# The first batch of an attention and mixture-of-experts kernel, taken by head groups

## The chip, the cores and the metric

The kernel runs on one core of a Trainium2 chip. The metric is the device time of one execution in microseconds (us). PE is TensorE, DVE is VectorE, ACT is ScalarE, POOL is GpSimd, and SP is the sync engine, which issues nearly all loads here.

## The reference

Three stages follow each other on 4 batches of 576 tokens with 8 heads of 64:

```
# 1. attention over 32 memory slots, per batch and head
a   = softmax over the 576 tokens of phi            # (576, 32)
k_m = a^T k ;  v_m = a^T v                          # (32, 64) each
att = softmax over the 32 slots of (q k_m^T / 8)    # (576, 32)
x   = att v_m                                       # heads side by side: 2304 x 512
# 2. dense MLP: h = x w_in ; x = (h * sigmoid(h)) w_out        (512 -> 2048 -> 512)
# 3. mixture of 8 experts, two per token: relu(x w1[e]) w2[e], weighted and summed
```

## The kernel before

The whole program is one stream of instructions per engine. The Python code names the steps; a scheduling layer sets each engine's order once, when the program is built, and `tc.issue_after` keeps a step from standing ahead of a named one. At run time every engine takes its own stream in order, and each instruction waits there for what it needs.

**Head groups.** Heads are taken in pairs `r` = 0 to 3. The index `g` splits the 8 heads in two groups of four, `g` = 0 and 1 (pairs 0, 1 and pairs 2, 3; the change's title calls them even and odd). Work on the 32 slots of four heads fills 128 partitions, so each step of attention comes as one piece per group.

**Batch 0 is the prologue.** For each group `phi_top` takes a maximum over token chunks (DVE, tile `mx`), `phi_max` finishes it through PE transposes (`mt`), subtracts it (DVE) and takes the exponential (ACT). `memory` multiplies it with keys and values (tile `kv`, and `kx` for the last, half chunk; 20 PE matmuls a group), sums the weights into `rs` and writes the scaled result to `src`. `memory_t` transposes `src` of both groups on PE into `kvt`. `scores` multiplies `kvt` with the queries `q`, two PSUM buffers (tag `aux`, of which there are two in all) for two groups; DVE transposes them into `sct`. `softmax_a` and `softmax_b` do the softmax (`smx`, `ssm`), `turn` transposes back (`att`), `halves` splits the result into a rounded part and a rest (both named `ah`). Tokens come in two ranges: 256 columns and 320 columns (`T0`, `TW`).

**The weights.** They arrive as 64-bit floats and are turned into 32-bit ones by ACT (`lw` and `wi` or `wo`) and two DVE steps, `join` (L217) and `sign` (L221); the raw pieces sit in four buffers `st`. `project` multiplies v_m into a slice of `w_in` (PE, `wph`, `wpl`), which saves the product with v_m later. `mlp_h` and `mlp_x` (L288, L313) are the dense MLP, in 32 steps a batch; the pieces of `w_in` and `w_out`, and the attention of the next batch, are hung on these steps by number.

**SP's queue.** Loads are issued in the order phi (both groups), kv and kx (pairs 0 to 3), the first 256 columns of q, two pieces of `w_in`, the rest of q, then further weights. A load also waits for the one eight places ahead of it and for its buffer.

Of the kernel before, what the change touches and what calls it, by code (L numbers as in the profile page):

```python
# [44 lines left out]
def body(ctx, tc, a):  # L45
# [36 lines left out]
    src = const.tile([128, 2, 2, 64], F32, name="src")  # L82

    def load_phi(b):
        PH[b] = ap_.tile([SC, NCH, 256], F32, name="phi", tag="big", bufs=1)
        if b:
            sp.dma_start(PH[b], a["phi"][b])
        else:
            load_phi_part(b, 0)
# [25 lines left out]
    def phi_max(b, g):
        r = slice(g * 128, (g + 1) * 128)
        pt = psum("aux", 2)
        pe.transpose(pt[:, :SC], MX.pop((b, g)), ident)
# [8 lines left out]
        return last

    def memory(b, g):
        pk = psum("aux", 2)  # L130
# [8 lines left out]
        dve.reciprocal(rs, rs)
        v, w = src[:, :, g, :], pk[:, :128].rearrange("p (t d) -> p t d", t=2)  # L140
        if b == 0:
            act.activation(v, w, AF.Copy, scale=rs)
        else:
            dve.tensor_scalar(v, w, rs, None, op0=OP.mult)

    def memory_t(b):
# [12 lines left out]
    def scores(b, i):  # L159
        t0, w = T0[i], TW[i]  # L160
        p = [psum("aux", 2)[:, :w] for g in range(2)]
        heads(p, b, 0, lambda h: QT[b, h][:, t0:t0 + w])
        if i == 0:
            AT[b] = ap_.tile([128, 2, S // M, M], F32, name="sct", tag="big", bufs=1)
        for g in range(2):
            dve.transpose(AT[b][:, g].rearrange("p a m -> p (a m)")[:, t0:t0 + w], p[g])

    def softmax_a(b, t0, w):
        n = w // M
        t = AT[b][:, :, t0 // M:t0 // M + n, :]  # L170
        mx = ap_.tile([128, 2, S // M], F32, name="smx")[:, :, :n]
# [5 lines left out]
    def softmax_b(b, t0, w):
        n = w // M
        t = AT[b][:, :, t0 // M:t0 // M + n, :]
        sm = ap_.tile([128, 2, S // M], F32, name="ssm")[:, :, :n]  # L180
# [844 lines left out]
def layout(inputs, np):  # L1025
# [45 lines left out]
```

## Time and profile before

| | |
|---|---|
| median of 3 runs | 845.61 us (845.02 to 845.68) |
| the profiled execution's own time | 845.91 us |
| its span, first to last instruction | 844.1 us |
| PE busy | 807.1 us, 96% of the span |
| DVE busy | 496.8 us, 59% |
| ACT busy | 360.8 us, 43% |
| POOL busy | 209.9 us, 25% |
| mean granted TensorE clock | 0.983 |
| DMA | 137.84 MB, 163 GB/s over the span |

The span divided in 40 slices of 21 us shows where PE is not full: in the first two slices its digits are 4 and 5, later 8 and 9. The granted clock (PEclk) reads 5 and 9 in the first two slices, then 9, the highest digit, throughout.

### The profile page before, as it was taken

The numbers are of one execution on the slowest core, as the hardware profiler recorded it, in microseconds if no ns is written. First come the engines' busy times: TensorE is split into PE (matmuls) and PEld (weight loads), VectorE is DVE, ScalarE is ACT, GpSimd is POOL, SyncE is SP. The second block draws the span as 40 slices with busy tenths as digits, with TensorE's granted clock in tenths as the row PEclk, the third lists the DMA queues.
The fourth block names the chain that finished last, engine by engine and source line by source line (L and its number), as shares of the span: only waits on it lengthen the run. The fifth ranks groups of instructions, "written<-read, shape, count | busy, mean of one in ns | idle before, by whom it ended". The sixth has DMA issues, their size and how long they took to land.

```text
span 844.1 us, 14185 instructions
## 1 busy us (share of the span) xinstructions
PE 807.1 (96%) x5260; PEld 691.4 (82%) x5260; DVE 496.8 (59%) x1178; ACT 360.8 (43%) x856; POOL 209.9 (25%) x237
## 2 busy tenths in 40 slices
PE   4589999999999999999999999999999999999996
PEld 2267678878887888887988989989989899898995
DVE  4898996884268747655724555354553654546521
ACT  3689975444333454553414433324332333233410
POOL 1254530021000400400541504215133142241301
PEclk9599999999999999999999999999999999999999
DMA  9889852543074215232456893765748647586201
GB/s 304 291 295 325 283 217 71 159 131 94 7 229 153 51 51 151 57 82 50 113 138 187 257 257 124 185 237 171 188 169 221 241 139 160 198 220 196 74 4 53
DMA packets 85935, 137.84 MB, mean 163 GB/s; under 512 B 14045, under 2 KB 48349, under 8 KB 85856
## 3 DMA queue, kind: packets, MB, share of 16 engines
q1 hardware_dynamic: 74656, 104.41, 40.9%
q0 software_dynamic: 11200, 32.43, 12.7%
q8 instruction: 43, 0.70, 0.4%
q14 instruction: 36, 0.29, 0.1%
HBM read 106.13 MB, written 31.26 MB: 163 GB/s over the span
## 4 chain that ended last, share of the span: by engine, by line
PE 81%; DVE 9%; ACT 4%; DMA 3%; issue 2%; POOL 1%; SPq 0%; POOLq 0%; ACTq 0%; DVEq 0%
PE x L706 25%; PE x L313 18%; PE x L682 13%; PE h L682 12%; PE h L288 9%; PE aux L157 2%; DMA st<-moe_w_out 1%; DVE th L293 1%; DVE gl L298 1%; DMA kx<-kx 1%; ACT lw L211 1%; POOL wo L232 1%; DMA st<-moe_w_in 1%; DVE mx L113 1%; DVE wo L217 1%
## 5 line engine op out<-in xcount | busy, mean ns | idle before, releaser
L706 PE MATMUL x<-w,gh 128*128 128x512 f32 (+1 forms) x608 | 188.1, 390 | 0.0
L706 PEld LDWEIGHTS x<-w,gh 128*128 128x128 f32 (+1 forms) x608 | 112.4, 186 | 24.3
L682 PE MATMUL h<-xh,w 128*128 128x304 f32 (+4 forms) x512 | 118.7, 304 | 0.0
L706 PE MATMUL x<-w,gl 128*128 128x512 f32 (+1 forms) x304 | 118.5, 390 | 0.0
L682 PE MATMUL x<-xh,w 128*128 128x304 f32 (+4 forms) x512 | 118.1, 302 | 0.0
L288 PE MATMUL h<-ah,wph 128*128 128x320 f32 (+1 forms) x512 | 109.3, 302 | 3.8 <-DVE th L293 1.7
L313 PE MATMUL x<-gh,woh 128*128 128x512 f32 x256 | 105.5, 412 | 0.0
L288 PEld LDWEIGHTS h<-ah,wph 128*128 128x128 f32 x512 | 90.0, 192 | 18.2 <-ACT ah L195 3.6
L721 POOL DMA_INDIRECT out<-y,tab x40 | 41.9, 1049 | 243.1 <-DVE y L716 187.3
L313 PE MATMUL x<-gl,woh 128*128 128x512 f32 x256 | 100.7, 393 | 0.7 <-DVE gl L298 0.7
L313 PE MATMUL x<-gh,wol 128*128 128x512 f32 x256 | 101.2, 395 | 0.0
L293 DVE SCALAR_TENSOR_TENSOR th<-th,h 128x256 f32<-128x256 f32 (+1 forms) x128 | 57.6, 450 | 53.0 <-ACT th L291 52.5
L497 POOL DMA_INDIRECT tab_d<-rows,slot x36 | 40.6, 1128 | 191.3 <-DVE slot L494 177.9
L682 PEld LDWEIGHTS h<-xh,w 128*128 128x128 f32 x512 | 87.3, 188 | 0.6
L682 PEld LDWEIGHTS x<-xh,w 128*128 128x128 f32 x512 | 87.4, 188 | 0.0
L291 ACT ACTIVATE th<-h 128x256 f32<-128x256 f32 (+1 forms) x128 | 52.3, 408 | 73.4 <-PE h L288 71.3
L288 PE MATMUL h<-ah,wpl 128*128 128x256 f32 (+1 forms) x256 | 76.6, 300 | 2.3 <-DVE wpl L264 2.3
L682 PE MATMUL x<-xl,w 128*128 128x304 f32 (+4 forms) x256 | 78.0, 305 | 0.0
L682 PE MATMUL h<-xl,w 128*128 128x304 f32 (+4 forms) x256 | 77.7, 303 | 0.0
L297 ACT ACTIVATE gh<-th 128x256 fp32r<-128x256 f32 x128 | 53.3, 416 | 55.7 <-DVE th L293 55.3
L298 DVE TENSOR_TENSOR gl<-th,gh 128x256 fp32r<-128x256 f32 x120 | 55.1, 459 | 32.0 <-ACT gh L297 28.1
L716 DVE SCALAR_TENSOR_TENSOR y<-x,tab,ex 128x512 f32<-128x512 f32 (+2 forms) x35 | 26.2, 749 | 71.4 <-PE x L706 71.4
(189 smaller groups left out, 1342.0 us busy)
## 6 DMA issues: line engine op xcount, KB each, us to landing
w2s<-moe_w SPq DMA_DIRECT2D x32, 512.0 KB, 8.5
wi<-win_d SPq DMA_DIRECT2D x24, 512.0 KB, 5.1
w1s<-moe_w SPq DMA_DIRECT2D x24, 512.0 KB, 6.2
kv<-kv SPq DMA_DIRECT2D x16, 520.0 KB, 7.3
st<-moe_w_in SPq DMA_DIRECT2D x16, 512.0 KB, 5.2
st<-moe_w_out SPq DMA_DIRECT2D x16, 512.0 KB, 5.9
xs_d<-ex SPq DMA_DIRECT2D x25, 256.0 KB, 3.6
x_d<-xs SPq DMA_DIRECT2D x36, 128.0 KB, 2.4
```

Of the source, the lines that this page charges most:

```text
L157: pe.matmul(p[g][h * M:(h + 1) * M], KVT[b][r, t, h * M:(h + 1) * M], moving(h)[r], start=True, stop=True)
L288: pe.matmul(p[:, :w], wt[:, g, c:c + 128], AH[b, g][at][:, t0:t0 + w], start=(n == 0), stop=(n == 5))
L291: act.activation(th[:, :w], p[:, :w], AF.Tanh, scale=0.5)
L293: dve.scalar_tensor_tensor(u[:, :w], th[:, :w], 1.0, p[:, :w], op0=OP.add, op1=OP.mult)
L297: act.activation(gh, u[:, :256], AF.Copy)
L298: last = (pool if b == 0 and (2 * f + i) % 4 == 0 else dve).tensor_sub(gl, u[:, :256], gh.bitcast(F32))
L313: pe.matmul(X2[key], held, moved, start=(f == 0 and n == 0), stop=(f == NF - 1 and n == 2))
L497: st = pool.indirect_dma_start(out=tab_d, out_offset=bass.IndirectOffsetOnAxis(ap=slot[:, j, k:k + 1], axis=0), in_=rows.bitcast(I32)[:, j ...
L682: pe.matmul(p[:, :w], wt[:, d, c], x[:, d, r], start=(n == 0), stop=(n == 11))
L706: mm = pe.matmul(p, g, w[:, f, :], start=(n == 0), stop=(n == (15 if both else 23)))
L716: done = dve.scalar_tensor_tensor(y, p[:P], w, EX[k, j], op0=OP.mult, op1=OP.add)
L721: st = pool.indirect_dma_start(out=a["out"], out_offset=bass.IndirectOffsetOnAxis(ap=TAB[k][:P, j, 0:1], axis=0), in_=y, in_offset=None, b ...
```

## The change

Batch 0 is taken group by group. SP's order becomes phi of group 0, kv and kx of pairs 0 and 1, phi of group 1, the first columns of q, kv and kx of pairs 2 and 3; the rest follows as before. phi lies group by group in memory, so that a half is one run of 2560 bytes per partition (before: five of 512). `memory_t`, `scores`, `softmax_a` and `softmax_b` take a list of groups; for the first 256 tokens they are called once per group, and group 0's softmax, `turn` and `halves` stand ahead of group 1's `memory`. The conversion of the first piece of `w_in` (`shrink`, `join`, `sign`) now stands behind group 1's `memory_t`. The scores of batch 0 use phi's buffer. Later batches load phi in two DMAs instead of one.

```diff
     load_phi(0)
+    for r in range(2):
+        load_kv(0, r)
     load_phi_part(0, 1)
     for r in range(4):
+        load_q(0, r, 0, T0[1])
+    for r in range(2, 4):
         load_kv(0, r)
-    for r in range(4):
-        load_q(0, r, 0, T0[1])
     fetch_win(0)
...
-    for g in range(2):
-        phi_top(0, g)
-        phi_max(0, g)
+    phi_top(0, 0)
+    phi_max(0, 0)
+    with tc.issue_after(MX["sub"].ins):
+        phi_top(0, 1)
     memory(0, 0)
-    memory(0, 1)
+    phi_max(0, 1)
+    memory_t(0, (0,))
+    scores(0, 0, (0,))
+    softmax_a(0, T0[0], TW[0], (0,))
+    softmax_b(0, T0[0], TW[0], (0,))
+    turned = turn(0, 0, T0[0], TW[0])
+    with tc.issue_after(turned.ins):
+        ready = memory(0, 1)
+    with tc.issue_after(ready.ins):
+        ready = halves(0, 0, T0[0], TW[0])
     first = ST.pop(("i", 0))
     WI[0] = m1.tile([128, 4, PW], F32, name="wi", tag="wi", bufs=2)
     parts = [WI[0][:, 2 * g:2 * g + 2, :].rearrange("p r f -> p (r f)") for g in range(2)]
-    narrow(first[0], parts[0], True)
-    memory_t(0)
-    scores(0, 0)
-    low = shrink(first[1], parts[1])
-    with tc.issue_after(softmax_a(0, T0[0], TW[0]).ins):
+    with tc.issue_after(ready.ins):
+        ready = memory_t(0, (1,))
+    turned = ready
+    with tc.issue_after(turned.ins):
+        low = shrink(first[0], parts[0])
+    scores(0, 0, (1,))
+    topped = softmax_a(0, T0[0], TW[0], (1,))
+    with tc.issue_after(topped.ins):
+        join(parts[0], low)
+    sign(first[0], parts[0])
+    with tc.issue_after(turned.ins):
+        low = shrink(first[1], parts[1])
+    with tc.issue_after(topped.ins):
         joined = join(parts[1], low)
     sign(first[1], parts[1])
     pool.dma_start(win_d[0], WI[0].rearrange("p r f -> p (r f)"))
     with tc.issue_after(joined.ins):
-        softmax_b(0, T0[0], TW[0])
-    turn(0, 0, T0[0], TW[0])
+        softmax_b(0, T0[0], TW[0], (1,))
     turned = turn(0, 1, T0[0], TW[0])
     project(0, 1)
-    halves(0, 0, T0[0], TW[0])
     ready = halves(0, 1, T0[0], TW[0])
```

The order of three engines shows it. On DVE, before, from the phi maxima to the first scores; `mx` is the maximum over chunks, `mt` the finished one, `rs` the sums of `memory`:

```order
L113 TENSOR_REDUCE mx<-phi 128x128 x2
L120 TENSOR_REDUCE mt<-aux 128x1
L125 TENSOR_TENSOR phi<-phi,aux 128x2x128
L125 TENSOR_TENSOR phi<-phi,aux 128x3x128
L120 TENSOR_REDUCE mt<-aux 128x1
L125 TENSOR_TENSOR phi<-phi,aux 128x2x128
L125 TENSOR_TENSOR phi<-phi,aux 128x3x128
L138 TENSOR_SCALAR rs<-aux 128x1
L139 RECIPROCAL rs<-rs 128x1
L138 TENSOR_SCALAR rs<-aux 128x1
L139 RECIPROCAL rs<-rs 128x1
```

The same place on DVE now (line numbers shift by a few; the score tile carries phi's name):

```order
L121 TENSOR_TENSOR phi<-phi,aux 128x256
L121 TENSOR_TENSOR phi<-phi,aux 128x384
L109 TENSOR_REDUCE mx<-phi 128x128
L134 TENSOR_SCALAR rs<-aux 128x1
L116 TENSOR_REDUCE mt<-aux 128x1
L135 RECIPROCAL rs<-rs 128x1
L121 TENSOR_TENSOR phi<-phi,aux 128x256
L121 TENSOR_TENSOR phi<-phi,aux 128x384
L167 STREAM_TRANSPOSE phi<-aux 128x256
L174 TENSOR_REDUCE smx<-phi 128x8
```

The second `mx` has moved behind the first group's subtraction, and the first group's reciprocal stands behind the second group's `mt`.

Further on, DVE now, from the end of group 0's softmax (`att`) to the weights of the first projection (`wi`):

```order
L190 STREAM_TRANSPOSE att<-phi 128x256
L134 TENSOR_SCALAR rs<-aux 128x1
L135 RECIPROCAL rs<-rs 128x1
L198 TENSOR_TENSOR ah_259<-att,ah_258 128x256
L167 STREAM_TRANSPOSE phi<-aux 128x256
L174 TENSOR_REDUCE smx<-phi 128x8
L175 TENSOR_TENSOR phi<-phi,smx 128x256
L219 SCALAR_TENSOR_TENSOR wi<-wi,lw 128x512
L223 SCALAR_TENSOR_TENSOR wi<-st,wi 128x512
L219 SCALAR_TENSOR_TENSOR wi<-wi,lw 128x512
L183 TENSOR_REDUCE ssm<-phi 128x8
L223 SCALAR_TENSOR_TENSOR wi<-st,wi 128x512
```

Group 1's `rs` stands behind the whole of group 0's softmax, and the four conversion steps stand behind group 1's scores; before, the first two of them stood ahead of the scores of both groups.

On PE, before, from the transposes of `src` to the first matmuls of the MLP:

```order
L149 MATMUL aux<-ident,src 128x128 x2
L157 MATMUL aux<-q,kvt 32x256 x8
L157 MATMUL aux<-wi,kvt 32x256 x8
L157 MATMUL aux<-q,kvt 32x320 x8
L288 MATMUL h<-ah_295,wph 128x256
```

The same place on PE now:

```order
L147 MATMUL aux<-ident,src 64x128 x2
L156 MATMUL aux<-q,kvt 32x256 x4
L132 MATMUL aux<-kv,phi 32x130 x16
L132 MATMUL aux<-kx,phi 32x130 x4
L147 MATMUL aux<-ident,src 128x128 x2
L156 MATMUL aux<-q,kvt 32x256 x4
L156 MATMUL aux<-wi,kvt 32x256 x8
L290 MATMUL h<-ah_258,wph 128x256
L290 MATMUL h<-ah_259,wph 128x256
L156 MATMUL aux<-q,kvt 32x320 x4
L290 MATMUL h<-ah_258,wpl 128x256
L156 MATMUL aux<-q,kvt 32x320 x4
```

The scores come four matmuls at a time instead of eight, and those of the second token range stand behind the projection and the first two MLP matmuls.

## Rows read from the trace of the kernel before

**Rows 1.** The page's chain that ended last, shares of the span by engine.

```profile
PE 81%; DVE 9%; ACT 4%; DMA 3%; issue 2%; POOL 1%; SPq 0%; POOLq 0%; ACTq 0%; DVEq 0%
```

**Rows 2.** Windows: stretch, length, busy PE, PEld, DVE, ACT, POOL; clock, DMA, GB/s.

```profile
0.00:28.50 28.50, 13.76 (x140) 7.17 (x141) 15.16 (x36) 9.63 (x20) 2.88 (x27) 0.81 0.87 289
28.50:45.00 16.50, 9.01 (x45) 5.80 (x44) 14.70 (x27) 13.13 (x29) 5.66 (x6) 0.61 0.93 304
45.00:75.00 30.00, 27.66 (x233) 21.04 (x233) 29.18 (x58) 26.73 (x64) 13.97 (x13) 1.00 0.89 303
75.00:90.00 15.00, 14.87 (x101) 11.51 (x102) 11.94 (x27) 13.49 (x33) 6.72 (x8) 1.00 0.98 333
90.00:120.00 30.00, 26.88 (x212) 19.84 (x211) 28.30 (x53) 26.12 (x61) 14.31 (x12) 1.00 0.68 237
120.00:844.10 724.10, 714.91 (x4536) 626.06 (x4534) 397.50 (x982) 271.69 (x654) 166.31 (x173) 1.00 0.49 143
```

**Rows 3.** Chain in order of time, first 30 us: start, us, what (DMA: issue to landing).

```profile
3.51 6.80 DMA kx<-kx
10.32 6.21 DMA st<-moe_w_in
```

**Rows 4.** Timeline, 4 to 16 us: start, busy, instruction, count, [idle before, releaser].

```profile
4.22 2.37 DVE L113 TENSOR_REDUCE mx<-phi 128x128 f32<-128x640 f32 x2 [3.22 <-DMA phi<-phi]
...
8.47 0.88 DVE L125 TENSOR_TENSOR phi<-phi,aux 128x256 f32<-128x256 f32 x2 [0.89 <-PE aux L122]
...
10.34 1.96 PE L136 MATMUL aux<-kv,phi 128*32 128x130 f32 x32
...
12.80 0.16 DVE L138 TENSOR_SCALAR rs<-aux 128x1 f32<-128x1 f32 x1 [1.47 <-PE aux L136]
...
13.35 1.32 PE L136 MATMUL aux<-kv,phi 128*32 128x130 f32 x26 [0.19 <-DMA kv<-kv]
...
15.50 0.37 ACT L142 ACTIVATE src<-aux,rs 128x128 f32<-128x128 f32 x1 [1.88 <-DVE rs L139]
...
15.92 0.44 PE L149 MATMUL aux<-ident,src 128*128 128x128 f32 x2 [0.92 <-ACT src L142]
```

**Rows 5.** Timeline, 16 to 28.5 us.

```profile
16.56 0.66 ACT L211 ACTIVATE lw<-st 128x512 int32<-128x512 uint32 x1 [0.69 <-DMA st<-moe_w_in]
...
17.67 0.37 ACT L151 ACTIVATE kvt<-aux 128x256 f32<-128x256 f32 x1
...
18.10 1.11 PE L157 MATMUL aux<-q,kvt 64*32 64x256 f32 x16 [1.74 <-ACT kvt L151]
...
19.32 0.78 DVE L166 STREAM_TRANSPOSE sct<-aux 128x256 f32<-128x256 f32 x2
...
20.13 0.69 DVE L172 TENSOR_REDUCE smx<-sct 128x16 f32<-128x512 f32 x1
...
22.93 1.08 PE L157 MATMUL aux<-wi,kvt 64*32 64x256 f32 x8 [1.70 <-DVE wi L221]
...
24.95 1.72 PE L157 MATMUL aux<-q,kvt 64*32 64x320 f32 x16 [0.94 <-DVE wpl L264]
...
27.95 0.51 DVE L166 STREAM_TRANSPOSE sct<-aux 128x320 f32<-128x320 f32 x1
```

**Rows 6.** Line L157 alone, 18 to 19.5 us: records, ns min/median/max, first and last start.

```profile
L157 PE MATMUL aux<-q,kvt x16: 630/632/633, 18.1 to 18.6; 64*32 64x256 f32 x16
```

**Rows 7.** Windows of 14.2 to 17.4 and 17.6 to 41.3 us, for the clock.

```profile
14.20:17.40 3.20, 1.24 (x30) 0.73 (x18) 0.32 (x2) 1.21 (x3) 0.00 (x0) 1.00 1.05 376
17.60:41.30 23.70, 12.74 (x82) 5.96 (x82) 20.38 (x40) 14.55 (x31) 4.64 (x5) 0.50 0.90 297
```

**Rows 8.** Timeline of DVE, 29 to 42 us.

```profile
29.25 0.81 DVE L172 TENSOR_REDUCE smx<-sct 128x20 f32<-128x640 f32 x1
...
36.52 0.91 DVE L188 STREAM_TRANSPOSE att<-sct 128x320 f32<-128x320 f32 x2 [0.83 <-POOL sct L184]
...
41.13 0.49 DVE L293 SCALAR_TENSOR_TENSOR th<-th,h 128x320 f32<-128x320 f32 x1 [0.76 <-ACT th L291]
```

More of the change, by code (lines that the diff above doesn't have):

```diff
@@ L84, in load_phi @@
     def load_phi(b):
[L85 to L89, printed above, removed]
+        PH[b] = ap_.tile([SC, 2, NCH * 128], F32, name="phi", tag="big", bufs=1)
+        for g in range(2) if b else (0,):
+            load_phi_part(b, g)
     def load_phi_part(b, g):
-        r = slice(g * 128, (g + 1) * 128)
-        sp.dma_start(PH[b][:, :, r], a["phi"][b][:, :, r])
+        sp.dma_start(PH[b][:, g], a["phi"][b, g])
     def load_kv(b, r):
@@ L109, in phi_top @@
     def phi_top(b, g):
-        r = slice(g * 128, (g + 1) * 128)
         mx = MX[b, g] = ap_.tile([SC, 128], F32, name="mx", bufs=2)
         with tc.issue_after(LATEST[0].ins) if b > 1 else ExitStack():
-            dve.tensor_reduce(mx, PH[b][:, :, r].rearrange("p c j -> p j c"), axis=AX.X, op=OP.max)
+            dve.tensor_reduce(mx, PH[b][:, g].rearrange("p (c j) -> p j c", c=NCH), axis=AX.X, op=OP.max)
     def phi_max(b, g):
-        r = slice(g * 128, (g + 1) * 128)
+        ph = PH[b][:, g].rearrange("p (c j) -> p c j", c=NCH)
         pt = psum("aux", 2)
@@ L123, in phi_max @@
         for c0, c1 in ((0, 2), (2, NCH)):
-            e = PH[b][:, c0:c1, r]
-            dve.tensor_sub(e, e, pb[:SC, None, :128].to_broadcast([SC, c1 - c0, 128]))
+            e = ph[:, c0:c1]
+            MX["sub"] = dve.tensor_sub(e, e, pb[:SC, None, :128].to_broadcast([SC, c1 - c0, 128]))
             last = act.activation(e, e, AF.Exp)
@@ L132, in memory @@
             for h in range(4):
-                j = (4 * g + h) * M
+                j = c * 128 + h * M
                 kv = KV[b, 2 * g + h // 2][:, c, h % 2, :] if c < 4 else KX[b, g][:, h % 2, :]
-                pe.matmul(pk[h * M:(h + 1) * M, :130], PH[b][:, c, j:j + M], kv, start=(c == 0), stop=(c == NCH - 1))
+                pe.matmul(pk[h * M:(h + 1) * M, :130], PH[b][:, g, j:j + M], kv, start=(c == 0), stop=(c == NCH - 1))
         rs = ap_.tile([128, 1], F32, name="rs", bufs=2)
@@ L141, in memory, with memory_t @@
         if b == 0:
[L142 to L146, printed above, removed]
+            return act.activation(v, w, AF.Copy, scale=rs)
+        return dve.tensor_scalar(v, w, rs, None, op0=OP.mult)
+    BOTH = (0, 1)
+    def memory_t(b, gs=BOTH):
         pt = psum("aux", 2)
+        r = slice(gs[0] * 64, gs[-1] * 64 + 64)
         for t in range(2):
-            pe.transpose(pt[:, t * 128:(t + 1) * 128], src[:, t].rearrange("p g d -> p (g d)"), ident)
-        KVT[b] = m1.tile([128, 2, 128], F32, name="kvt", bufs=2)
-        act.activation(KVT[b].rearrange("p t j -> p (t j)"), pt[:, :256], AF.Copy)
@@ L153, in heads @@
-    def heads(p, b, t, moving):
+            pe.transpose(pt[:r.stop, t * 128:(t + 1) * 128], src[:, t, :gs[-1] + 1].rearrange("p g d -> p (g d)"), ident)
+        if b not in KVT:
+            KVT[b] = m1.tile([128, 2, 128], F32, name="kvt", bufs=2)
+        return act.activation(KVT[b][r].rearrange("p t j -> p (t j)"), pt[r, :256], AF.Copy)
+    def heads(p, b, t, moving, gs=BOTH):
         for h in range(4):
-            for g in range(2):
+            for g in gs:
                 r = slice(g * 64, (g + 1) * 64)
@@ L157, in heads, with scores @@
                 pe.matmul(p[g][h * M:(h + 1) * M], KVT[b][r, t, h * M:(h + 1) * M], moving(h)[r], start=True, stop=True)
-    def scores(b, i):
+    def scores(b, i, gs=BOTH):
         t0, w = T0[i], TW[i]
[L161 to L171, printed above, removed]
+        p = {g: psum("aux", 2)[:, :w] for g in gs}
+        heads(p, b, 0, lambda h: QT[b, h][:, t0:t0 + w], gs)
+        if b not in AT:
+            t = PH[b] if b == 0 else ap_.tile([128, 2, NCH * SC], F32, name="sct", tag="big", bufs=1)
+            AT[b] = t[:, :, :S].rearrange("p g (a m) -> p g a m", m=M)
+        for g in gs:
+            last = dve.transpose(AT[b][:, g].rearrange("p a m -> p (a m)")[:, t0:t0 + w], p[g])
@@ L172, in softmax_a @@
+        return last
+    def softmax_a(b, t0, w, gs=BOTH):
+        n, c = w // M, len(gs)
+        t = AT[b][:, gs[0]:gs[-1] + 1, t0 // M:t0 // M + n, :]
+        mx = ap_.tile([128, 2, S // M], F32, name="smx")[:, :c, :n]
         dve.tensor_reduce(mx, t, axis=AX.X, op=OP.max)
-        last = dve.tensor_sub(t, t, mx[:, :, :, None].to_broadcast([128, 2, n, M]))
+        last = dve.tensor_sub(t, t, mx[:, :, :, None].to_broadcast([128, c, n, M]))
         act.activation(t, t, AF.Exp, scale=0.125)
@@ L175, in softmax_a, with softmax_b @@
         return last
[L177 to L180, printed above, removed]
+    def softmax_b(b, t0, w, gs=BOTH):
+        n, c = w // M, len(gs)
+        t = AT[b][:, gs[0]:gs[-1] + 1, t0 // M:t0 // M + n, :]
+        sm = ap_.tile([128, 2, S // M], F32, name="ssm")[:, :c, :n]
         dve.tensor_reduce(sm, t, axis=AX.X, op=OP.add)
@@ L183, in softmax_b @@
         dve.reciprocal(sm, sm)
-        (pool if b == 0 and t0 else dve).tensor_mul(t, t, sm[:, :, :, None].to_broadcast([128, 2, n, M]))
+        (pool if b == 0 and t0 else dve).tensor_mul(t, t, sm[:, :, :, None].to_broadcast([128, c, n, M]))
     def turn(b, g, t0, w):
@@ L852, in body @@
     fetch_win(1)
-    for g in range(2):
-        phi_top(0, g)
-        phi_max(0, g)
+    phi_top(0, 0)
+    phi_max(0, 0)
+    with tc.issue_after(MX["sub"].ins):
+        phi_top(0, 1)
     memory(0, 0)
-    memory(0, 1)
+    phi_max(0, 1)
[8 more added lines that the diff above has]
+        ready = halves(0, 0, T0[0], TW[0])
     first = ST.pop(("i", 0))
@@ L1036, in layout @@
     ph[:, :, 4, :, 1] = np.roll(ph[:, :, 4, :, 1], 64, axis=1)
-    ph = ph.reshape(B, SC, NCH, H * M)
+    ph = ph.reshape(B, SC, NCH, 2, 4 * M).transpose(0, 3, 1, 2, 4).reshape(B, 2, SC, NCH * 4 * M)
     arrays = {"qt": qt, "kv": np.ascontiguousarray(kv[:, :, :4]), "kx": np.ascontiguousarray(kx),
```

## The prediction

> **What bounds the kernel now.** I read the chain by engine first: PE holds 81% of it, DVE 9%, ACT 4%, DMA 3% [rows 1]. The windows then show where the rest lies [rows 2]. From 120 us to the end PE is busy 714.9 of 724.1 us; nothing there is touched. In the first 28.5 us PE is busy 13.8 and DVE 15.2: this is latency, a chain of short steps. From 28.5 to 75 us DVE is the full engine (14.7 of 16.5, then 29.2 of 30), from 75 to 90 it is PE (14.9 of 15), from 90 to 120 DVE again (28.3 of 30). So the change is worth what it moves the moment from which DVE is full, less what later idle time takes up. I measure that moment at DVE's second transpose of the 320-column scores, which ends at 27.95 + 0.51 = 28.46 [rows 5].
>
> Two waits in front of it are the change's targets. Loads run without a gap: kx of pair 1 lands at 3.51 + 6.80 = 10.31, the first `w_in` piece at 10.32 + 6.21 = 16.53 [rows 3]. And ACT copies `kvt` only after it has waited 0.69 for that piece and converted it [rows 5].
>
> **The loads.** Between 10.31 and 13.35, when PE's wait for kv ends [rows 3, 4], two kv pieces of 520 KB came in: 2.9 ns a KB, an estimate that gives 0.94 for half of phi, 0.38 for kx and 1.5 for the first columns of q. In the new order as many bytes stand up to group 1's phi as stood up to kx before, so it lands at 10.3. kx of group 0 comes at 9.4 and its last kv at 9.0, q at 11.8, group 1's kv at 14.9, the `w_in` piece at 16.5 as before. Longer runs for phi may make its halves cheaper, by something between 0 and the 0.94 itself; no row shows it, and I take 0, since every other load keeps its form. On SP the kv loads of group 1 now wait for those of group 0 (queue places), which land by 9.4, while SP still has loads in flight up to 11.8: hidden. Later, two kv loads of batch 1 stand ahead of two `w_in` pieces, and these wait for the moved `sign`, so they come some 4 us later; ACT used the like not before 29 us, behind a piece that is there already, so I cost this at nothing, and at one landing's delay, 1.3, if that is wrong.
>
> **Group 0.** `mx` takes 2.37 / 2 = 1.19 and ends at 5.4; before, 6.59 (4.22 + 2.37) to 8.47 passed until the first subtraction, 1.88 [rows 4]. So it starts at 7.3 and the exponentials end about 8.8. PE then waits for the kv of 9.0, and `memory` takes 10.34 to 12.80, 2.46: `rs` at 11.5. DVE's queue holds group 1's `mx` first, 10.3 to 11.5, so nothing is lost there. But the reciprocal stands behind `mt` of group 1, which needs a PE transpose: about half of the 1.88, so 12.4. Behind it come `src` 0.37; PE, which has group 1's second phi matmul until 11.5 + 1.9 = 13.4 in front; the transposes (0.44 at the full clock, I take 0.6 at the half); `kvt` 0.37 [rows 4, 5]: 14.4. Scores cost 1.22 from PE's start to DVE's (18.10 to 19.32) with eight matmuls [rows 5]. For four I take the same: sixteen records of 0.63 fit in 1.11, so they ran side by side, and leaving half out need not shorten the rest [rows 5, 6]; 0.6, in proportion, is the other end. [...] DVE starts on group 0's scores at 15.6.
>
> **The half softmax.** A reduction takes 0.69 over 512 and 0.81 over 640 elements a partition [rows 5, 8]: 0.94 ns an element and 0.21 fixed. Five steps over 256 then take 0.45 each, two small ones 0.21, two transposes 0.39 to 0.45: 3.5, with handoffs 3.6, so group 0 is through at 19.2. Seven steps are there twice; DVE's six of them cost 6 x 0.21 = 1.3 more in all. [...]
>
> **Group 1.** Its kv is multiplied by 17.4, but `rs` and the reciprocal stand behind group 0's last transpose: 19.6. `src`, transposes, `kvt`, scores: 0.37 + 0.6 + 0.37 + 1.22 and 0.2 of handoffs, 22.4; before, DVE had the scores of both at 19.32. Transpose and the two steps of `softmax_a`: 23.7. The four conversion steps, 0.69 each as the equally wide reduction, and one `ssm` between them: 26.9. Before, PE's projection, which waits for the last of them, began at 22.93 [rows 5]. From there to the 320-column scores it took 2.02, to 24.95: now 28.95. These are two passes of 1.4 where 24.95 to 26.67 was one, the first 0.4 sooner for it needs one buffer alone. The second transpose ends near 28.95 - 0.4 + 2.8 + 0.5 = 31.9. **DVE's full stretch starts 3.4 us later**: 1.3 of it repeated fixed cost, the rest waiting between the groups, with the conversions no longer under it. In DVE's full queue behind it this delays every weight that PE waits for.
>
> **What is given back.** DVE idles 0.83 for POOL's multiplication and 0.76 for ACT's tanh [rows 8]. In the new order a `sign` and a `join` stand between reciprocal and transpose, and ACT has more ready: I take both, 1.6. PE's idle 2.3 between 45 and 75 and 3.1 between 90 and 120 [rows 2] could take more, but DVE is full there and is what PE waits for; none. The sum against the profiled execution's own time is 845.91 + 3.4 - 1.6 = 847.7. That run is 0.30 above the median of the runs, so I say **847.4**. The later batches' second phi load hides under PE (full from 120 us); if not, it costs at most the 0.94 of a half load three times, 2.8.
>
> **The rivals.** [...]
>
> *Nothing is left of it.* PE's idle 5.4 after 45 us takes up the 1.8: 845.6. DVE's idle 3.1 in 75 to 90 [rows 2] speaks for it, its full stretches on both sides against.
>
> *Dearer.* On PE half of the third projection now stands ahead of an MLP step and waits for DVE's rests of the second. If the lag is not given back and PE's run, which had brought the clock back by 41.3 [rows 7], starts 3.4 later in pieces, half the clock over that stretch costs some 1.7 again: 845.61 + 3.4 + 1.7 = 850.7. Against it: PE is idle there anyway.
>
> **How the numbers follow.** Forecast (846.4 to 849) 0.45; clock, faster, 0.20; nothing left 0.23; dearer 0.12. What a measurement can tell from no change is 0.2%, 1.7 us: slower means above 847.3. The forecast gives slower 0.33 and same 0.12, the dear case slower 0.12, nothing left same 0.21 and slower 0.02, the clock faster 0.18 and same 0.02. Together faster 0.18, same 0.35, slower 0.47. The range of 843.9 to 849.8 leaves out half of the dear case and a tenth of the clock's; the forecast's own is 846.4 to 849.
>
> **What would show it.** Group 0's scores at DVE near 15.6 and its `att` near 19; group 1's scores at DVE after 22; the projection after 26.5; the second 320-column transpose near 32; DVE's idle before the 320-column `att` gone; granted clock 0.50 in 20 to 40. The prediction is wrong if `memory` of group 0 ends much before 11 or the projection starts before 24.

## The result, and the profile after

The changed kernel takes 852.40 us (median of 4 runs, 852.19 to 852.70), the kernel before beside it 845.64 (845.02 to 846.64): 6.8 us slower by the medians, a ratio of 1.0085 with a 95% interval of 1.0072 to 1.0098. The profiled execution took 852.7, with a span of 850.9. The page's chain by engine reads almost as before [rows 1] and hides the difference; windows do not. Stretch, length, busy PE, PEld, DVE, ACT, POOL; clock, DMA, GB/s, of the changed kernel:

```profile
0.00:28.50 28.50, 14.26 (x132) 7.04 (x132) 15.18 (x39) 9.31 (x20) 2.87 (x27) 0.85 0.87 283
28.50:45.00 16.50, 9.24 (x56) 4.73 (x48) 13.85 (x25) 11.21 (x23) 4.82 (x5) 0.50 0.93 297
45.00:75.00 30.00, 27.65 (x163) 21.98 (x159) 26.60 (x51) 25.25 (x62) 12.77 (x12) 0.91 0.80 279
75.00:90.00 15.00, 14.22 (x152) 11.17 (x145) 12.51 (x30) 13.19 (x31) 6.41 (x7) 1.00 0.88 302
90.00:120.00 30.00, 27.05 (x204) 20.73 (x203) 26.00 (x48) 26.05 (x60) 14.91 (x14) 1.00 0.79 277
120.00:850.90 730.90, 719.70 (x4583) 628.23 (x4582) 404.06 (x995) 276.14 (x668) 165.34 (x174) 1.00 0.49 142
```

Against [rows 2], DVE is no longer full where it was: from 45 to 75 us it is busy 26.6 instead of 29.2, from 90 to 120 26.0 instead of 28.3. It is idle 4.9 us more in these 60 us. (A window cuts both programs at the same times, not at the same work, so this is a sign and not yet a sum.) What DVE waits for there is ACT. The longest of its waits in the changed kernel, 45 to 75 us and then 90 to 122 (who waited for whom, us in total, times, longest):

```profile
DVE th L295 <- ACT th L293: 3.1, 2, 2.1
```

```profile
DVE th L295 <- ACT th L293: 1.3, 2, 1.0
DVE wol L278 <- ACT woh L277: 1.3, 2, 0.7
DVE ssm L183 <- ACT sct L176: 1.2, 1, 1.2
```

In the kernel before, the same view lists one wait of DVE from 45 to 75, of 0.2, and three from 90 to 122, of 0.9, 0.7 and 0.2.

The prologue came out near the forecast at its end, less so on the way. Timeline of the changed kernel, 14 to 32 us (start, busy, instruction, count, [idle before, releaser]):

```profile
14.62 0.45 DVE L167 STREAM_TRANSPOSE phi<-aux 128x256 f32<-128x256 f32 x1 [1.27 <-PE aux L156]
15.10 0.42 DVE L174 TENSOR_REDUCE smx<-phi 128x8 f32<-128x256 f32 x1
...
17.88 0.45 DVE L190 STREAM_TRANSPOSE att<-phi 128x256 f32<-128x256 f32 x1
...
19.99 1.08 PE L156 MATMUL aux<-q,kvt 64*32 64x256 f32 x8 [0.47 <-ACT kvt L150]
...
21.14 0.45 DVE L167 STREAM_TRANSPOSE phi<-aux 128x256 f32<-128x256 f32 x1 [1.34 <-PE aux L156]
...
25.55 1.08 PE L156 MATMUL aux<-wi,kvt 64*32 64x256 f32 x8 [0.50 <-DVE wi L223]
...
27.11 0.80 PE L290 MATMUL h<-ah,wph 128*128 128x256 f32 x2 [0.49 <-DMA st<-moe_w_in]
...
27.84 1.29 PE L156 MATMUL aux<-q,kvt 64*32 64x320 f32 x8
...
29.06 0.58 PE L290 MATMUL h<-ah,wpl 128*128 128x256 f32 x1
...
29.57 1.29 PE L156 MATMUL aux<-q,kvt 64*32 64x320 f32 x8
...
31.01 0.52 DVE L167 STREAM_TRANSPOSE phi<-aux 128x320 f32<-128x320 f32 x1 [0.91 <-PE aux L156]
```

The last row ends at 31.53; before it was 28.46 [rows 5]. That is a lag of 3.1 where 3.4 was forecast. Not all of it is the prologue's: MLP matmuls (`h`) stand ahead of the two passes of 320-column scores and between them, and that belongs to the new order of the queues (see e1).

The clock is the other thing that meets the eye. Windows chosen at its steps, changed kernel:

```profile
16.50:19.80 3.30, 0.60 (x7) 0.20 (x2) 2.30 (x8) 0.91 (x3) 0.00 (x0) 1.00 1.05 385
20.00:41.00 21.00, 10.07 (x62) 2.93 (x62) 16.82 (x33) 12.94 (x26) 4.81 (x5) 0.50 0.85 261
41.20:50.50 9.30, 9.28 (x36) 7.61 (x37) 6.94 (x16) 6.43 (x15) 3.79 (x5) 0.50 0.91 307
50.70:54.00 3.30, 3.30 (x19) 2.90 (x18) 2.00 (x5) 2.96 (x8) 0.86 (x2) 1.00 1.00 362
```

In the kernel before the clock was at 0.50 up to 41.3 [rows 7] and at 1.00 in the window from 41.5 to 60 (PEclk reads 9 and 5 in the page's first two slices, not 5 and 9: 0.92 from 0 to 21 us, 0.51 from 21 to 42); here PE works through 9.3 us without a gap (9.28 busy) at 0.50 before it rises.

To see where the lag grows, I took the start of ACT's tanh of each MLP step from the timelines, this kernel minus before, in us (before: step 0 at 32.39, step 34 at 133.78):

| step | changed | e1: old order behind 27 us | e2: only that order new | e3: changed, clock early |
|---|---|---|---|---|
| 0 | 3.33 | 1.84 | 2.70 | 3.67 |
| 4 | 4.37 | 2.35 | 3.49 | 1.92 |
| 7 | 2.81 | 1.83 | 1.93 | 1.58 |
| 16 | 5.41 | 1.79 | 4.81 | 4.39 |
| 24 | 4.39 | 2.03 | 4.60 | 3.82 |
| 28 | 7.25 | 2.04 | 7.01 | 6.28 |
| 34 | 6.97 | 2.03 | 6.72 | 6.01 |

Each column is one execution; the changed kernel traced again (e16) reads 2.46 at step 0 and 5.92 at step 34. From step 30 on the changed kernel's lag holds, at 6.8 to 7.0, to the end. In the changed kernel it is 2.8 at step 7 (55.6 us before), after the stretch at half the clock, and grows later: about 2.6 by step 16 and, after some is given back, 2.9 between steps 24 and 28 (2.6 from 24 to 34). The later columns are the experiments.

### The profile page after: what moved, and what is told of

Read it like the earlier page. It is cut to its first block, busy times and chain, and to the rows that moved or that the text cites. A ratio compares the mean times of both kernels' runs of the same rounds, so it can differ in the third digit from the quotient of the medians.

```text
span 850.9 us, 14217 instructions
## 1 busy us (share of the span) xinstructions
PE 812.1 (95%) x5262; PEld 693.9 (82%) x5262; DVE 498.2 (59%) x1184; ACT 361.1 (42%) x858; POOL 207.1 (24%) x237
## 4 chain that ended last, share of the span: by engine, by line
PE 81%; DVE 9%; ACT 3%; DMA 3%; issue 1%; POOL 1%; SPq 0%; POOLq 0%; ACTq 0%
PE x L708 25%; PE x L315 18%; PE x L684 12%; PE h L684 12%; PE h L290 9%; PE aux L156 2%; DMA kv<-kv 2%; POOL wo L234 1%; DMA st<-moe_w_in 1%; DVE gl L300 1%; DVE th L295 1%; DVE mx L109 1%; DVE wo L219 1%; ACT lw L213 1%; DVE wi L219 1%
## 5 line engine op out<-in xcount | busy, mean ns | idle before, releaser
L290 PEld LDWEIGHTS h<-ah,wph 128*128 128x128 f32 x512 | 91.1, 194 | 17.4 <-ACT ah L197 2.6
```

Source lines behind the costliest of these rows:

```text
L290: pe.matmul(p[:, :w], wt[:, g, c:c + 128], AH[b, g][at][:, t0:t0 + w], start=(n == 0), stop=(n == 5))
```

## The experiments

Ratios are to the kernel before, run beside each on the same chip. Beside e13 to e18 all kernels, before too, took 3 to 6 us longer (before: 850.71 for e13 to e16, 848.79 for e17 and e18), so ratios are compared and not times. The last column is the ratio less one, times 845.

| run | ratio | 95% interval | us by the ratio |
|---|---|---|---|
| changed kernel | 1.0085 | 1.0072 to 1.0098 | +7.2 |
| e1 old order behind 27 us | 1.0021 | 1.0012 to 1.0031 | +1.8 |
| e2 only the order new | 1.0087 | 1.0073 to 1.0101 | +7.4 |
| e3 changed, unread matmuls | 1.0079 | 1.0065 to 1.0093 | +6.7 |
| e4 before, unread matmuls | 0.9994 | 0.9985 to 1.0003 | -0.5 |
| e5 late rows old | 1.0051 | 1.0037 to 1.0065 | +4.3 |
| e6 early rows old | 1.0068 | 1.0054 to 1.0081 | +5.7 |
| e7 all old but SP | 1.0068 | 1.0054 to 1.0082 | +5.7 |
| e8 all new but SP | 1.0094 | 1.0079 to 1.0109 | +7.9 |
| e9 one ACT row | 1.0075 | 1.0063 to 1.0087 | +6.3 |
| e10 filled prologue, old order | 1.0003 | 0.9994 to 1.0013 | +0.3 |
| e11 before, two edits | 0.9988 | 0.9980 to 0.9997 | -1.0 |
| e12 ACT's late rows old | 1.0179 | 1.0166 to 1.0192 | +15.1 |
| e13 four places | 1.0087 | 1.0069 to 1.0105 | +7.4 |
| e14 e10 with unread matmuls | 0.9997 | 0.9983 to 1.0012 | -0.3 |
| e15 e10, the scheduler's order | 1.0065 | 1.0049 to 1.0081 | +5.5 |
| e16 changed kernel again | 1.0105 | 1.0089 to 1.0121 | +8.9 |
| e17 e14 again | 1.0004 | 0.9995 to 1.0013 | +0.3 |
| e18 e11 again | 0.9989 | 0.9980 to 0.9998 | -0.9 |

**The tool: hold the order.** The scheduler sets each engine's order from the whole program, so an edit of the first 27 us also changes the queues behind it. To part the two, the instructions from the 320-column scores to step 36 are chained, engine by engine, in a listed order (the code there is traced alike in both kernels):

```diff
+    START = len(nc.cur_bb.bb.instructions)
     with tc.issue_after(turned.ins):
         scores(0, 1)
...
+    PLACES = {"PE": "0 1 2 3 4 5 6 7 8 9 10 11 12 13 26 27 ...", "DVE": "...", "Activation": "...", "Pool": "...", "SP": "..."}
+    def hold():
+        now = nc.cur_bb.bb.instructions[START:]
+        for e, text in PLACES.items():
+            mine = [i for i in now if str(i.engine) == "EngineType." + e]
+            places = [int(x) for x in text.split()]
+            for x, y in zip(places, places[1:]):
+                tc.add_manual_dep(mine[y], mine[x].name,
+                                  mybir.DependencyInfo(mybir.DependencyClass.NoSync, mybir.DependencyReason.DATA),
+                                  reason="hold")
...
     def run_hooks(s):
+        if s == 36:
+            hold()
```

The edge only fixes the order of issue and waits for nothing. A kernel chained in its own order has the queues that it had: e3 and e4 below are chained so, with unread matmuls besides, and stand at 1.0079 and 0.9994 beside the 1.0085 and 1 of the kernels that they were made from.

**e1 and e2: prologue and order crossed.** e1 is the changed kernel with the places of before, e2 the kernel before with the places of the changed one.

> The changed kernel's code for the first batch up to 27 us, and behind it, from the 320-column scores to step 36, every engine's queue in the order that the kernel before has there. Theory Q (the scheduler gave the queues behind the change another order, above all ACT's conversions, and that costs PE waits at 60 to 120 us): only the lag of the prologue is left, 845.6 + 3.1 = 848.7, between 848.0 and 849.6. Theory C (the half clock, which lasts 9.2 us longer, cost the rest): 852.4 again, 851.5 to 853. Theory L (the lag alone grows by itself to 6.8): 852.4 as well.

> The kernel before with its own first 27 us, and behind it the changed kernel's order of every queue up to step 36. Theory Q: 845.6 + (6.8 - 3.1) = 849.3, between 848 and 850.5. Theories C and L: no change, 845.2 to 846.4.

e1 took 847.45 against 845.31, e2 852.77. With the old order the changed prologue costs 1.8 (1.0 to 2.6), by the ratio, and its lag stays at 1.8 to 2.0 from step 0 on. The old prologue with the new order costs as much as the whole change, 7.4: its lag starts at 2.7 already, since the new order puts MLP matmuls in front of the 320-column scores (its first scores had reached DVE at 18.39, 0.9 sooner than in the trace of before), and then it grows as in the changed kernel. So the order alone makes the loss, and under it the lag of the prologue adds nothing that can be measured. Theory Q holds against C and L, in direction and not in size: e1 came 0.6 below its range and e2 2.3 above, so the two effects, 1.8 and 7.4, do not simply add up.

The prologue's own lag is smaller than 3.1. Up to the projection e1 and the changed kernel run alike (second pass at 25.54 and 25.55), and then e1's transposes, without the MLP matmuls in front, end at 29.69 + 0.91 = 30.60, 2.1 behind the kernel before:

```profile
29.69 0.91 DVE L167 STREAM_TRANSPOSE phi<-aux 128x320 f32<-128x320 f32 x2 [0.92 <-PE aux L156]
```

Windows of e1 show DVE as full again as in the kernel before:

```profile
45.00:75.00 30.00, 28.81 (x208) 22.41 (x211) 29.32 (x58) 26.43 (x63) 14.51 (x13) 0.95 0.88 293
90.00:120.00 30.00, 26.99 (x197) 20.17 (x183) 28.23 (x52) 27.34 (x64) 15.25 (x14) 1.00 0.71 251
```

**e3 and e4: the clock.** 37 (e3) and 28 (e4) matmuls of ready operands, written to a PSUM tile that nobody reads, are put in PE's idle stretches; all queues keep their own order.

```diff
+    spin = psum("x2", 4)
+    SPIN = [pe.matmul(spin[:, :256], AH[0, 0][0][:, :128], AH[0, 0][0][:, :256], start=True, stop=True).ins
+            for _ in range(37)]
```

> The changed kernel with 37 matmuls of 128x256 that nobody reads, in PE's idle stretches between 31.8 and 41.2 us (20, 8 and 9 of them); all other queues keep their order. The granted clock should be back at 1.00 before 41 us instead of at 50.6. Theory C: the 9.4 us of MLP that ran at half the clock shrink to about 5.1, so 852.4 - 3.7 = 848.7. Theory Q: the lag is 2.8 us at step 7 (58 us) although the clock came only at 50.6, so little is to be had: 852.4, not under 851.4.

> The kernel before with 28 such matmuls in PE's idle stretches at 29.2 to 34.1 us and 36.5 to 37.6 us. Granted clock back at 1.00 by about 36 instead of 41.4. Theory C: 3.3 us of MLP at 37.6 to 40.8 shrink by 1.6, so 844.0. Theory Q: DVE is full there and hides it, 845.6, between 845.0 and 846.2.

PE was fast again early. Eight matmuls of the projection in e3, before the unread matmuls and behind the first of them, then eight in the changed kernel:

```profile
25.87 1.08 PE L156 MATMUL aux<-wi,kvt 64*32 64x256 f32 x8 [0.46 <-DVE wi L223]
...
36.38 0.64 PE L156 MATMUL aux<-wi,kvt 64*32 64x256 f32 x8 [1.20 <-DVE wi L223]
```

```profile
36.05 1.08 PE L156 MATMUL aux<-wi,kvt 64*32 64x256 f32 x8 [4.24 <-DVE wi L223]
```

Windows of e3 (the clock of 1.00 in the first does not fit the 1.08 at 25.87, so for the time before the unread matmuls the durations are the better witness):

```profile
20.00:41.00 21.00, 14.67 (x99) 8.16 (x99) 16.48 (x32) 13.08 (x26) 4.48 (x5) 1.00 0.82 248
41.20:50.50 9.30, 8.48 (x49) 6.57 (x50) 8.07 (x20) 8.39 (x21) 4.52 (x5) 1.00 0.96 345
...
45.00:75.00 30.00, 27.17 (x188) 21.54 (x187) 26.84 (x52) 25.86 (x62) 13.16 (x13) 0.94 0.84 297
90.00:120.00 30.00, 27.07 (x195) 20.15 (x194) 25.57 (x46) 26.05 (x60) 15.80 (x14) 0.94 0.75 257
```

PE had all of 41.2 to 50.5 at 1.00, and still DVE has its idle time behind it, and the ratio is 1.0079 against 1.0085, with intervals that overlap. What the half clock cost is 0.5 by the ratios, 1.0 by the traces at step 34 (6.97 - 6.01), and with 1.0065, the low end of e3's interval, 1.7; not 3.7. Theory C falls; it looked plausible because 9.3 us of the lead engine at a clock of 0.50 are easy to see, while DVE's missing 4.9 us are spread over 60. In e4 the gain, 0.5, can't be told from nothing; its time, 844.71, lies between the two forecasts.

**e5 to e8: where in the order.** All four are the changed kernel with mixed places. The places divide at about 60 us (PE's 135th, DVE's 62nd, ACT's 54th row) where both orders have issued the same instructions. In short form:

```diff
-    PLACES = new
+    PLACES = {e: new[e][:CUT[e]] + old[e][CUT[e]:] for e in new}  # e5
+    PLACES = {e: old[e][:CUT[e]] + new[e][CUT[e]:] for e in new}  # e6
+    PLACES = {**old, "SP": new["SP"]}  # e7
+    PLACES = {**new, "SP": old["SP"]}  # e8
```

> The changed kernel; queue order as changed up to some 60 us (PE's 135th row behind the 27 us, DVE's 62nd, ACT's 54th), from there to step 36 as in the kernel before. Theory late (the rows from 60 to 120 us, batch 1's attention among weight conversions, make the loss): 847.5 as with all rows in the old order, between 846.8 and 849. Theory early (the rows from 27 to 60 us, where half of the third projection and the loads moved, make it): 852.4, not under 851. If both have a share: between.

> The complement: the changed kernel with the rows from 27 to about 60 us in the order of before, and those from 60 us to step 36 as changed. Theory late: 852.4, not under 851. Theory early: 847.5, between 846.8 and 849.

> The changed kernel with PE, DVE, ACT and POOL in the order of before from 27 us on, and only SP (the loads: two kv loads of batch 1 in front of two w_in pieces, and so on) in the changed order. Theory loads (late weight pieces make the loss): 850 to 852.8. Theory compute queues: 847.5, between 846.8 and 848.3. The prediction priced the moved loads at 0 or 1.3: 847.5 or 848.8.

> The complement: the changed kernel with its own order on PE, DVE, ACT and POOL, and SP's loads from 27 us on in the order of before. Theory loads: 847.5 to 849. Theory compute queues: 852.4, not under 851.

The late rows have a share: with the early rows old (e6) 5.7 is left, 3.9 more than the 1.8 of e1, and at step 34 of the traces 4.38 against 2.03. The early rows' share is less sure. With the late rows old (e5) 4.3 is left, 2.5 more than in e1, and the two intervals do not overlap; but they come from two sets of runs, by its own time (848.74) e5 lies in theory late's range, and its trace, taken of its fastest run, has only 2.41 at step 34. DVE's idle time follows the half that is new. Windows of e5, then of e6:

```profile
45.00:75.00 30.00, 27.98 (x190) 22.56 (x190) 26.96 (x54) 25.69 (x63) 13.15 (x13) 0.94 0.81 284
90.00:120.00 30.00, 28.08 (x207) 21.19 (x205) 28.23 (x52) 27.61 (x64) 15.62 (x14) 1.00 0.77 267
```

```profile
45.00:75.00 30.00, 26.72 (x195) 20.35 (x194) 28.30 (x53) 25.48 (x60) 13.82 (x13) 1.00 0.87 293
90.00:120.00 30.00, 25.99 (x194) 19.26 (x193) 25.62 (x48) 26.05 (x61) 15.26 (x14) 1.00 0.72 252
```

The loads show what an order is. With the old order on the other engines, SP's new one costs 1.0068 against 1.0021, 4.0 us: batch 1's phi lands later, and the reduction of it stands in DVE's queue where it used to be ready. DVE in e7, then the same row in e1:

```profile
52.77 1.23 DVE L109 TENSOR_REDUCE mx<-phi 128x128 f32<-128x640 f32 x1 [3.37 <-DMA phi<-phi]
```

```profile
49.44 1.32 DVE L109 TENSOR_REDUCE mx<-phi 128x128 f32<-128x640 f32 x1
```

PE in e7 waits for the product that stands behind that reduction in DVE's queue, and its lag grows from 2.3 at step 4 to 5.3 at step 7:

```profile
54.39 0.71 PE L315 MATMUL x<-gl,woh 128*128 128x512 f32 x1 [3.05 <-DVE gl L300]
```

But in the changed kernel the old loads mend nothing (e8, 1.0094): there DVE waits for ACT. Neither theory of the pair holds by itself; a queue is early or late only against the others.

**e9, e12 and e13: single places.** e9 swaps two rows of ACT, e13 moves rows at four places, e12 gives ACT alone the old order behind 60 us.

In the list of ACT's places 162 is batch 1's exponential and 191 a conversion `wo<-st`; 151 and 152 are two `wph<-aux`, 156 a conversion, 150 a `gh<-th`. In DVE's, 137 and 138 are the `wpl` of these, 135 a `th`, 143 a `wol` and 144 a transpose of scores. e9, then what e13 has besides:

```diff
-    "Activation": "... 161 163 191 162 164 ..."
+    "Activation": "... 161 163 162 191 164 ..."
```

```diff
-    "Activation": "... 149 156 150 148 151 152 158 ..."
+    "Activation": "... 149 151 152 156 150 148 158 ..."
-    "DVE": "... 133 135 142 136 137 138 139 143 144 ..."
+    "DVE": "... 133 137 138 135 142 136 139 144 143 ..."
```

> The changed kernel with every queue in its own order but for one swap on ACT: the exponential of batch 1 (128x1152) in front of one w_out conversion (wo<-st), where it stands behind it. In the changed kernel ACT waits 0.87 for POOL with that conversion, and DVE's next reduction waits 1.25 for the exponential. Theory Q (single places in the queues make the late loss): 851.2, between 850.6 and 851.8. If PE does not depend on that place: 852.4.

> The changed kernel in its own order but for four places between 105 and 120 us: on ACT the projection's two copies (wph) in front of a w_out conversion and a gh that waits for DVE, and batch 1's exponential in front of a conversion that waits for POOL; on DVE the projection's two subtractions (wpl) in front of a tanh step, and the first transpose of batch 1's second scores in front of a wol that waits for ACT. The lag to the kernel before grows there from 4.4 to 7.0. If these places make it: 852.4 - 2.2 = 850.2, between 849.4 and 851.2. If the loss sits elsewhere in the late rows: 852.4, not under 851.6.

> The changed kernel with only ACT's rows from 60 us to step 36 in the order of before; PE, DVE, POOL, SP keep the changed order. With all late rows old it was 3.9 over before instead of 6.8 to 7. If ACT's queue is what makes the late loss: 849, between 848 and 850. If it is DVE's or the loads': 852.4, not under 851.

What a bad place looks like, in the changed kernel: ACT, POOL and DVE, 116 to 122 us.

```profile
118.62 0.68 ACT L214 ACTIVATE wo<-st 128x512 f32<-128x512 f32 x1 [0.87 <-POOL wol L278]
119.21 1.15 ACT L176 ACTIVATE sct<-sct 128x1152 f32<-128x1152 f32 x1
```

```profile
116.65 1.94 POOL L278 TENSOR_TENSOR wol<-wo,woh 128x512 fp32r<-128x512 f32 x1 [0.74 <-ACT woh L277]
```

```profile
116.08 1.35 DVE L175 TENSOR_TENSOR sct<-sct,smx 128x1152 f32<-128x1152 f32 x1
...
120.39 1.35 DVE L183 TENSOR_REDUCE ssm<-sct 128x36 f32<-128x1152 f32 x1 [1.25 <-ACT sct L176]
```

The exponential needs nothing from POOL. It stands behind a conversion that waits for POOL to let go of a buffer, and DVE waits for the exponential. Its own input was done at 117.43 (DVE L175, 116.08 + 1.35), and still ACT sat idle from 117.75 to 118.62: it took the two in the order of its queue. In e1 the same conversion stands ahead of the same exponential and costs nothing, since POOL's `wol` came at 111.28:

```profile
114.40 1.17 ACT L176 ACTIVATE sct<-sct 128x1152 f32<-128x1152 f32 x1 [0.49 <-DVE sct L175]
```

The swap in e9 removed DVE's wait:

```profile
119.68 1.34 DVE L183 TENSOR_REDUCE ssm<-sct 128x36 f32<-128x1152 f32 x1
```

From step 24 to 34 the lag then grew by 1.5 instead of 2.6, but it had reached 5.3 instead of 4.4 by step 24 in that execution, and the ratio, 1.0075, can't be told from the changed kernel's (the time, 851.49, is in theory Q's range, but the kernel before beside it took 844.65 and not 845.64). In e13, PE's wait of 1.90 for `wpl` at 109.62 went down to 0.23, and a new one stood at 116.77. The changed kernel, then e13:

```profile
109.62 1.10 PE L156 MATMUL aux<-q,kvt 64*32 64x320 f32 x16 [1.90 <-DVE wpl L266]
```

```profile
107.92 1.10 PE L156 MATMUL aux<-q,kvt 64*32 64x320 f32 x16 [0.23 <-DVE wpl L266]
...
116.77 0.51 PE L290 MATMUL h<-ah,wph 128*128 128x256 f32 x2 [1.53 <-DVE th L295]
```

Its ratio, 1.0087, lies 0.0018 under that of the changed kernel on the same chip (e16, 1.0105), with intervals that overlap: unclear, and from step 24 to 34 its lag grew by 1.7, where the changed kernel's grew by 2.6 and 2.1 (e16): most of the 2.2 did not come. e12 is the plainest of all: ACT's late rows in the order that was good in the kernel before, with the changed order on the others, is the slowest kernel of the study, +15.1, which neither of its forecasts had. So I found no single place that holds the late loss; which places make it up stays open.

**e10, e14, e15, e17: another prologue by head groups.** e10 fills DVE's idle time between the groups: group 1's `memory` no longer waits for group 0's `turn`, and ACT takes group 1's `kvt` and the first conversions there. It has the old order behind; e15 leaves that order to the scheduler; e14 and e17 add 27 unread matmuls to e10.

```diff
     softmax_a(0, T0[0], TW[0], (0,))
-    softmax_b(0, T0[0], TW[0], (0,))
-    turned = turn(0, 0, T0[0], TW[0])
-    with tc.issue_after(turned.ins):
-        ready = memory(0, 1)
-    with tc.issue_after(ready.ins):
-        ready = halves(0, 0, T0[0], TW[0])
+    memory(0, 1)
...
-    with tc.issue_after(ready.ins):
-        ready = memory_t(0, (1,))
-    turned = ready
+    turned = memory_t(0, (1,))
     with tc.issue_after(turned.ins):
         low = shrink(first[0], parts[0])
+    softmax_b(0, T0[0], TW[0], (0,))
+    turn(0, 0, T0[0], TW[0])
     scores(0, 0, (1,))
...
+    halves(0, 0, T0[0], TW[0])
```

> The changed kernel with the old order behind the 27 us, and group 1's memory no longer held back behind group 0's softmax; group 1's copy of keys and values and the first conversions come in DVE's idle time between the groups. With the old order alone it was 847.4, 1.8 to 2.1 over before. If the lag came from the idle time between the groups (about 1.4 of DVE's 2.6 idle us there can be filled): 845.9, between 845.0 and 846.8. If loads or the repeated fixed cost set it: 847.4.

> The filled prologue with the old order (845.0 alone, its 320-column scores 1.6 us earlier than in the kernel before), and 27 unread matmuls in PE's idle stretches at 27.6 to 32.5 and 34.9 to 36.0 us. As in the kernel before, where they gave 0.7: 844.3, between 843.4 and 845.2. Rival: the wait behind step 16 takes it, 845.

> The filled prologue of e10, and the order of the queues behind it left to the scheduler. Theory Q (the loss is the order that the scheduler draws up, not the prologue): it is slower than with the old order, 845.0, by 2 to 8, so 847 to 853. Theory P (the changed prologue's lag makes the loss, and filling it mends it): 845 to 846.

> e14 once more on another chip: there a wait of 1.9 us at 344 to 346, in a part that no kernel changes, and times that spread over 6 us hid what it is worth; its trace stood 3.0 us ahead of the kernel before at step 34. If that lead stays: 842.6 where the kernel before takes 845.3, ratio 0.9965 to 0.998. If it is a wash as measured: 0.999 to 1.001.

e10's two 320-column transposes end at 26.23 + 0.91 = 27.14, where the kernel before had 28.46:

```profile
26.23 0.91 DVE L167 STREAM_TRANSPOSE phi<-aux 128x320 f32<-128x320 f32 x2 [0.93 <-PE aux L156]
```

So the groups can be ahead, by 1.3 in that execution. At the end nothing can be told from no change: 1.0003, and with unread matmuls 0.9997 and 1.0004. In e10's trace half of a lead of 1.7 is gone behind step 16. e15, the same prologue with the scheduler's order, is 1.0065: 5.2 us over e10, though on another chip. Theory Q has it again, with a prologue that has no lag: from step 0 to 34 e15's lag grows from -0.14 to 3.40, e10's from -1.62 to -0.87. (e14 and e17 differ by 2.1 at step 0 as traced, -1.60 and 0.53: that much the first 30 us can vary between two executions of one kernel. The record gives both the same chip number, though e17's forecast speaks of another chip.)

**e16, the changed kernel again,** on the chip of e13 to e15:

> The changed kernel once more, as it is, beside the others on the same chip: 852.4, between 851.8 and 853.

It took 858.44 where before took 850.71. The ratio is 0.0020 over the first one: two sets of runs of one kernel can differ by that much, so steps between sets that are smaller than this show nothing by themselves.

**e11 and e18: a version that beats both.** The kernel before with 28 unread matmuls and the small steps of the first softmax ahead of the projection's subtractions on DVE, its own order held behind:

```diff
-        softmax_b(0, T0[0], TW[0])
-    turn(0, 0, T0[0], TW[0])
-    turned = turn(0, 1, T0[0], TW[0])
-    project(0, 1)
+        scaled = softmax_b(0, T0[0], TW[0])
+    with tc.issue_after(scaled.ins):
+        last = project(0, 1)
+    with tc.issue_after(last.ins):
+        turn(0, 0, T0[0], TW[0])
+        turned = turn(0, 1, T0[0], TW[0])
```

> The kernel before with the 28 unread matmuls of the earlier run (that alone: 844.7) and one more move on DVE: the small steps and the multiplication of the first softmax go ahead of the projection's two subtractions, for which DVE waits a microsecond at 23.5. Expected: the second transpose of the 320-column scores 0.6 earlier, 844.0, between 843.3 and 844.8, so faster than both kernels by about 1.3 and 8. Rival: PE's pass for these scores starts later by 0.2 and sets the end: 844.8 or more.

> e11 once more beside it, to see which of the two is the faster: ratio 0.9988 again, between 0.998 and 0.9997. Its trace lost at steps 6 to 17 the 1.9 us that it was ahead.

0.9988 (843.67 against 844.65) and 0.9989: faster than the kernel before by about 1 us twice, and than the changed one by some 8. Which of the two edits gives it is not shown; the unread matmuls alone (e4) could not be told from nothing.

## Why the prediction was wrong

**The sum for the prologue: the difference right, both terms too large.** Group 0's scores came to DVE at 14.6 (15.6 forecast) and group 1's at 21.1 (22.4); the second pass of the projection at 25.6 (26.9), and the second 320-column transpose ended at 31.5 (31.9). So the groups were 1.0 to 1.3 early, and the stretch behind them was longer by about 1.0, for the MLP matmuls in front of and between the score passes, which the sum did not count. (Of the signs named for being wrong one came by a hair, the projection's first half at 23.98 where 24 was the bound; it says nothing of the loss.) The prologue's own lag is the 2.1 of e1, not 3.4. "What is given back", 1.6, is next to nothing in e1: the lag is 2.1 at the transposes, 1.84 at step 0 and 2.03 at step 34, and DVE still waits 0.83 for POOL and 0.75 for ACT's tanh. In the changed kernel the first of these waits is gone, as forecast, and the second is 0.96. DVE in e1, then in the changed kernel:

```profile
38.37 0.90 DVE L190 STREAM_TRANSPOSE att<-phi 128x320 f32<-128x320 f32 x2 [0.83 <-POOL phi L186]
...
42.97 0.49 DVE L295 SCALAR_TENSOR_TENSOR th<-th,h 128x320 f32<-128x320 f32 x1 [0.75 <-ACT th L293]
```

```profile
39.99 0.89 DVE L190 STREAM_TRANSPOSE att<-phi 128x320 f32<-128x320 f32 x2
...
44.76 0.49 DVE L295 SCALAR_TENSOR_TENSOR th<-th,h 128x320 f32<-128x320 f32 x1 [0.96 <-ACT th L293]
```

From PE's start to DVE's, four score matmuls took 21.14 - 19.99 = 1.15 where eight took 1.22 [rows 5], so the end that was taken was right and the proportional 0.6 wrong. A half reduction took 0.42, with 0.69 for a whole one [rows 5]: 1.05 ns an element and 0.15 fixed, where 0.94 and 0.21 were taken. Six repeats then cost 0.9, an estimate from these rows, and not 1.3.

**Right, but for another kernel, and by luck: 847.4.** "The sum against the profiled execution's own time is 845.91 + 3.4 - 1.6 = 847.7" is the time of e1, 847.45: the changed prologue with the old order behind it. The 1.8 of e1 is the forecast's 3.4 less 1.6 because both terms were too large by nearly the same.

**The step that failed** is the one that carried the lag to the end: "In DVE's full queue behind it this delays every weight that PE waits for." It took the stretch from 28.5 to 120 us from the kernel before, DVE full and its queue the same, only later. In the changed kernel all five queues there have another order, and DVE is no longer full: it waits for ACT. No term of the sum priced that. The runs put 5.4 us on it under the new prologue (changed kernel less e1) and 7.4 under the old one (e2). The changed order was seen in three places and each was priced by itself as it would fall into the old queues: half a projection ahead of an MLP step (in a rival), two kv loads ahead of two pieces of `w_in` (at nothing, or 1.3), ACT's "more ready" (as a gain). The second has a measured price now, 4.0 in the old queues (e7) and none in the new ones (e8).

**The rivals.** *Dearer* had the direction and the wrong mechanism: it added 1.7 for the half clock. The clock did stay low, 9.2 us longer, but e3 puts that at 0.5 to 1.0. A clock that is high early, with a faster kernel, had a chance of 0.20 and didn't come: the granted clock was 0.50 from 20 to 50.5 us, and 1.00 (50.7 to 54) only behind 9.3 us of unbroken work. *Nothing left of it* is what e10 measured, with another prologue.

**What stays open:** which rows make the 5 us. The late rows have a share by ratio and trace, the early rows by the ratio; four named places do not account for the late part. In the early rows one wait stands out that no run tested alone: PE waits 1.8 for DVE's `mt` of batch 1 in the changed kernel and 1.9 in e5, 0.7 in the kernel before and in e1.

## What to carry to other kernels

Where a scheduler sets the order of the queues, an edit has two effects: what it does where it stands, and the order that it makes of everything behind. The second was three times the first here, and was nothing that the diff shows; hold the old order for one run before a change is judged. Do not price a moved instruction in the old queues: ask which queues still fit one another, and look in the profile for a stretch in which an engine that was full has come to wait.

## What was not expected of the hardware

- Nine microseconds of PE at half its clock cost 0.5 to 1.0 us (e3). By the traces e3 was 2.4 ahead of the changed kernel at step 4 and 1.0 from step 16 on; where the rest went is not shown.
- The mean granted clock of a run says nothing on its time here: the four runs of the changed kernel have 0.981, 0.995, 0.976 and 0.997, and times from 852.19 to 852.70. It is also to be read with care: a window can show 1.00 where the matmuls in it take as long as at 0.50 (e3, 1.08 at 25.87).
- One engine's order put back to what was good, alone, made the changed kernel slower by 7.9 us more (e12, 1.0179 against 1.0085): as much again as the whole change.
